# Network two by seven products: other places for the products in the spare bank, the output sums, the copies of TI and the loads of W7

## The chip, the cores and the metric

The kernel runs on one core of a Trainium2 chip. The metric is device time in microseconds (us). Engines: PE is TensorE (matmuls), DVE is VectorE, ACT is ScalarE, POOL is GpSimd, SP is the engine whose queue issues nearly all DMAs. SBUF is the on-chip memory and PSUM, which the matmuls write, is used here as eight banks of 128 x 512 float32.

## What is computed

Three parts follow each other: a two-dimensional Fourier transform (its real part), a gated network ("network one") and a second network ("network two"):

```
def _moe2_ref(x, w_in, w_out):
    h = x @ w_in                  # 12288 x 256 @ 256 x 2048
    g = h - np.tanh(h)
    return (g @ w_out)            # 12288 x 2048 @ 2048 x 256
```

The change touches network two and the last steps of network one ahead of it.

## The kernel before

Tokens are taken in 12 blocks of 1024 (`n` = 0 to 11), the 2048 hidden columns in 8 steps of 256 (`q` = 0 to 7). In a step the product with `w_in` is a 2 x 2 block product done with seven products in place of eight (the names `a11`, `a12`, `a22`, `s1` to `s4`). Each product of a 128 x 128 weight with 512 tokens in float32 is three matmuls (`mm3`, lines 395 to 397). The product with `w_out` is taken two steps at a time: for an even step (`seven` in the code, called a seven step here) it is again seven products, with sums of the weight `W7` and of the activations; for an odd step it is eight plain ones (`whole`, with the weight `WO`), six matmuls for each of the blocks "11", "12", "21" and "22". Block 0 uses an older routine (`quad`, with plain products only); blocks 1 to 11 use `step`.

The eight PSUM banks: `x0` and `x1` (used in turn by the steps), `z`, `w` (a step's work) and four outputs `o00`, `o01`, `o10`, `o11`. In a step the bank `x` of the other parity is first still read by the step before (DVE turns its content into operands, the rows `m<-x` and `s<-x`), and then free until the next step begins: `apart` uses it as spare bank (tile `k`) for those of the seven products that belong to two outputs. Four of the seven (`a11`, `s1`, `s2`, `s3`) go there; `add` then puts `k` into an SBUF sum `acc` (a copy by ACT for the first one of a block, line 1015, a DVE addition after that, line 1017), and the next step's first product can start in the bank when that is done. The other three go straight to an output bank (`direct`). After the last step of a block, `joined` adds the four sums up on POOL (lines 1024 to 1027) and `ready` adds an output bank to each and stores it (lines 1031 to 1034). A block's last products are made in step 0 and step 1 of the next block: `joined` at the end of step 0, `ready` in step 1, right behind the last product of the outputs.

Every engine takes its instructions in the order of the code. Work that belongs to no step (the split of the next block's operands, the loads and splits of weights) is written into numbered slots, four for a step (`at`), and `fill` puts the next slot's work into the program at four places of each step; slot `16 * NP` is the first of network two. Names of that work: `weights2` loads `w_in` (tile `wf`), splits it into `TI` and `w_out` into `WO`, and stores `TI` in DRAM (`ti<-TI`), from where `stream` loads it again for later blocks; `seven` loads and splits `W7`; `left2` loads the next block's activations (`xk<-spill`).

## Time and profile before

| what | value |
|---|---|
| time, median of 3 runs | 1729.41 us (1728.98 to 1732.79) |
| profiled execution, its own time | 1735.3 us |
| span in the profiled execution | 1733.5 us |
| PE busy | 1653.2 us, 95% |
| DVE busy | 1284.5 us, 74% |
| ACT busy | 1214.2 us, 70% |
| POOL busy | 1101.9 us, 64% |
| mean granted TensorE clock | 0.98 |

A busy PE counts overlapped matmuls, each with a modelled end; whether it runs at its rate is read from the distance of the starts. "Idle before" an instruction is the time that its engine had nothing to do ahead of it, and the name behind the arrow is what ended it.

### The profile page before, as it was taken

To read this page: it belongs to the slowest core of one execution; us is meant where nothing else is said; L and a number is where in the kernel's file an instruction comes from. 1 tells how busy PE (TensorE), PEld (TensorE's weight loads), DVE (VectorE), ACT (ScalarE), POOL (GpSimd) and SP (SyncE) were. 2 spreads that over 40 slices of the span, in tenths; PEclk is the share of its full clock that TensorE was granted. 3 is DMA by queue.
4 is the path that set the end of the run, shared out by engine and by line. 5 is a ranking of instruction groups with operands and counts; after the bars stand their busy time and mean duration, and the time that the engine had idled before them with its cause. 6 is when DMAs were issued, how large, how long until landed. Compare 5 with 4: busy or idle time off the path is not lost.

```text
span 1733.5 us, 22370 instructions
## 1 busy us (share of the span) xinstructions
PE 1653.2 (95%) x7346; PEld 1331.8 (77%) x7346; DVE 1284.5 (74%) x1979; ACT 1214.2 (70%) x2333; POOL 1101.9 (64%) x913
## 2 busy tenths in 40 slices
PE   8999999999999999899998999999999999999997
PEld 7978888888888887677776777777767777777775
DVE  7987888888988976667676767666666666676766
ACT  5887777777777766777676767676757676767664
POOL 1166666667767664957575757585757575667644
PEclk9999999999999999999999999999999999999999
DMA  9610111121111134352323232323232333323220
GB/s 330 158 52 26 44 61 44 43 68 49 50 37 43 55 132 136 134 197 86 131 88 112 89 130 86 134 85 121 98 114 98 103 107 106 109 88 131 80 94 25
DMA packets 58341, 167.97 MB, mean 97 GB/s; under 512 B 6752, under 2 KB 14944, under 8 KB 58224
## 3 DMA queue, kind: packets, MB, share of 16 engines
q1 hardware_dynamic: 56640, 162.08, 27.3%
q0 software_dynamic: 1440, 4.46, 1.5%
q8 instruction: 58, 0.95, 0.2%
q14 instruction: 59, 0.48, 0.1%
q10 hardware_dynamic: 144, 0.00, 0.0%
HBM read 127.65 MB, written 38.86 MB: 96 GB/s over the span
## 4 chain that ended last, share of the span: by engine, by line
PE 66%; DVE 9%; issue 8%; POOL 7%; ACT 6%; DMA 2%; SPq 1%; POOLq 0%; DVEq 0%; ACTq 0%
PE o L396 9%; PE o L395 9%; PE o L397 9%; PE x L395 6%; PE x L396 5%; PE x L397 5%; PE w L395 2%; PE w L397 2%; PE w L396 2%; DVE acc L1017 2%; PE k L395 2%; POOL a L1058 2%; PE k L397 2%; PE k L396 2%; ACT s L1056 1%
## 5 line engine op out<-in xcount | busy, mean ns | idle before, releaser
L1058 POOL TENSOR_TENSOR a<-g,a 128x512 fp32r<-128x512 f32 x132 | 171.1, 1296 | 195.9 <-ACT a L1056 193.6
L696 POOL TENSOR_TENSOR a<-xk,a 128x512 fp32r<-128x512 f32 x70 | 93.0, 1333 | 149.3 <-ACT a L694 149.3
L1058 POOL TENSOR_TENSOR s<-g,s 128x512 fp32r<-128x512 f32 x132 | 170.8, 1294 | 13.5 <-ACT s L1056 13.5
L395 PE MATMUL o<-m,WO 128*128 128x512 f32 x416 | 162.7, 391 | 0.0
L396 PE MATMUL o<-m,WO 128*128 128x512 f32 x416 | 162.5, 391 | 0.0
L397 PE MATMUL o<-m,WO 128*128 128x512 f32 x416 | 162.4, 390 | 0.0
L1048 ACT ACTIVATE c<-z 128x512 f32<-128x512 f32 x176 | 106.0, 602 | 71.6 <-DVE z L1089 43.4
L696 POOL TENSOR_TENSOR s<-xk,s 128x512 fp32r<-128x512 f32 x94 | 125.4, 1334 | 39.4 <-ACT s L694 36.1
L396 PE MATMUL o<-m,wv 128*128 128x512 f32 x384 | 150.1, 391 | 0.1
L397 PE MATMUL o<-m,wv 128*128 128x512 f32 x384 | 150.0, 391 | 0.0
L395 PE MATMUL o<-m,wv 128*128 128x512 f32 x384 | 150.0, 391 | 0.0
L1158 POOL TENSOR_TENSOR g<-g,g 128x512 f32<-128x512 f32 x88 | 113.6, 1290 | 46.4 <-DVE x L1157 42.3
L1056 ACT CAST a<-g 128x512 fp32r<-128x512 f32 x132 | 82.1, 622 | 60.0 <-DVE g L1094 31.7
L1052 ACT COPY s<-x 128x512 f32<-128x512 f32 x176 | 103.3, 587 | 18.6 <-PE x L397 18.2
L1017 DVE TENSOR_TENSOR acc<-acc,k 128x512 f32<-128x512 f32 x132 | 89.9, 681 | 33.9 <-PE k L397 33.1
L571 ACT ACTIVATE c<-z 128x512 f32<-128x512 f32 x112 | 67.2, 600 | 54.4 <-DVE z L660 53.6
L578 DVE TENSOR_TENSOR m<-z,m 128x512 fp32r<-128x512 f32 x112 | 76.8, 686 | 37.5 <-ACT m L576 37.5
L1056 ACT CAST m<-z 128x512 fp32r<-128x512 f32 x88 | 51.8, 589 | 67.0 <-DVE z L1118 57.2
L395 PE MATMUL x<-a,TI 128*128 128x512 f32 x192 | 81.1, 422 | 14.6 <-ACT acc L1015 8.0
L396 PEld LDWEIGHTS o<-m,WO 128*128 128x128 f32 x416 | 78.3, 188 | 17.1 <-DVE m L578 0.3
L395 PEld LDWEIGHTS o<-m,WO 128*128 128x128 f32 x416 | 78.1, 188 | 17.0
L397 PEld LDWEIGHTS o<-m,WO 128*128 128x128 f32 x416 | 78.2, 188 | 16.8
(278 smaller groups left out, 5436.9 us busy)
## 6 DMA issues: line engine op xcount, KB each, us to landing
TI<-ti SPq DMA_DIRECT2D x88, 896.0 KB, 4.7
spill<-r SPq DMA_DIRECT2D x48, 256.0 KB, 2.6
xk<-spill SPq DMA_DIRECT2D x48, 256.0 KB, 6.3
out<-acc SPq DMA_DIRECT2D x44, 256.0 KB
ti<-TI SPq DMA_DIRECT2D x8, 896.0 KB, 4.7
raw<-w_in SPq DMA_DIRECT2D x32, 128.0 KB, 2.3
cv<-w_out SPq DMA_DIRECT2D x16, 256.0 KB, 3.1
wf<-wf SPq DMA_DIRECT2D x16, 256.0 KB, 5.0
```

What stands on the lines that cost most here:

```text
L395: T.matmul(ps, w[0], m[0], start=start, stop=False, skip_group_check=True)
L396: T.matmul(ps, w[0], m[1], start=False, stop=False, skip_group_check=True)
L397: T.matmul(ps, w[1], m[0], start=False, stop=stop, skip_group_check=True)
L571: A.activation(t, src, ACT.Tanh if ph == 2 else ACT.Relu)
L578: V.tensor_sub(M[blk][:, 1], g, M[blk][:, 0].bitcast(F32))
L696: eng.tensor_sub(S[name][:, 1], src(), S[name][:, 0].bitcast(F32))
L1017: self.V.tensor_add(self.acc[key], self.acc[key], K)
L1048: A.activation(t, src, TANH)
L1052: A.copy(t, src)
L1056: A.copy(M[k][:, 0], src)
L1058: eng.tensor_sub(M[k][:, 1], src, M[k][:, 0].bitcast(F32))
L1158: "+s2": lambda: G.tensor_sub(g("22"), g("22"), g("11")), "+s4": lambda: G.tensor_sub(g("12"), g("12"), g("22")),
```

## The change

In `step`, products in the spare bank are made at other places in the order of PE and their sums at other places in the order of DVE: in a seven step `s3` comes ahead of the step's own `s3` product and `s2` right behind `s1`, in an odd step `a11` comes ahead of the own `s3` and `s1` right behind `s1`. The first sum is a copy by DVE in place of ACT. `joined` stands ahead of the split of `a22` on POOL. The two outputs of `ready` are taken later in step 1: the lower pair behind the first half's operand, the upper pair behind the second half's. The block's first straight products `a22` and `a12` are made in step 2 and no longer in step 1. The three first stores `ti<-TI` move by 7 to 12 slots into block 0, and the loads and splits of `W7` move from slots 10 to 27 of network two to slots 18 to 50, with the tile `wf` of `weights2` in place of one of the four `xt`.

```diff
--- before.py
+++ after.py
@@ -919,7 +919,7 @@
         return u
 
     def weights2(self, slot, q, pool, tag, bufs):
-        a, b = [], []
+        a, b, out = [], [], []
         def load(to, pool, tag, bufs, i):
             def f():
                 to.append(pool.tile([128, TOK], F32, tag=tag, name="wf", bufs=bufs))
@@ -931,21 +931,22 @@
             f, g = self.quad_weights(self.p2a, self.TI[q])
             f(a[0])
             b.append(g)
+            out.append(self.TI[q])
         def wo():
             p, t = (self.p2a, f"WO{q}") if q < 4 else (self.wvp, "wv")
             self.WO[q] = p.tile([128, 2, TOK], F32R, tag=t, name="WO", bufs=1 if q < 4 else 4)
             self.split(self.WO[q], b[1], self.V if q < 2 else self.G)
         def keep():
-            b[0](None)
-            self.nc.sync.dma_start(out=self.ti[q], in_=self.TI[q].rearrange("p s k n -> p (s k n)").bitcast(F32))
-        self.at(slot, load(a, self.p2a, "wf", 1, 4 + q), ti, None, None, None, keep)
+            self.nc.sync.dma_start(out=self.ti[q], in_=out[0].rearrange("p s k n -> p (s k n)").bitcast(F32))
+        self.at(slot, load(a, self.p2a, "wf", 1, 4 + q), ti, None, None, None, lambda: b[0](None))
+        self.at(16 * NP + ((5, 6, 10)[q] if q < 3 else 4 * q - 3), keep)
         self.at(slot + 4, load(b, pool, tag, bufs, 12 + q), None, wo)
 
     def seven(self, slot, q):
 
         src, t, i = [], [], q // 2
         def load():
-            src.append(self.kp.tile([128, TOK], F32, tag="xt", name="wf", bufs=4))
+            src.append(self.p2a.tile([128, TOK], F32, tag="wf", name="wf", bufs=1) if q else self.kp.tile([128, TOK], F32, tag="xt", name="wf", bufs=4))
             for to, at, n in ((0, 128, 128), (128, 0, 128), (256, 256, 256)):
                 self.nc.sync.dma_start(out=src[0][:, to:to + n], in_=self.wf[12 + q, :, at:at + n])
         def first():
@@ -953,7 +954,7 @@
             f, g = self.quad_weights(self.p2b, self.W7[q])
             f(src[0])
             t.append(g)
-        self.at(slot, load, None, first, None, None, lambda: t[0](None))
+        self.at(slot, load, None, first, None, None, None, lambda: t[0](None))
 
     def bank(self, tag, name):
         return self.ps.tile([128, TOK], F32, tag=tag, name=name, bufs=1)
@@ -987,8 +988,6 @@
         t = int(blk[0]) - 1
         for h in range(2):
             self.into(p["n"], t, h, [c[s][:, 128 * h:128 * h + 128] for s in range(2)], p["m"][blk])
-        if p["q"] == 7 and blk in ("21", "12"):
-            self.ready(p["n"], t)
 
     def product(self, w, k):
 
@@ -1012,7 +1011,7 @@
             key = w["n"], k
             if key not in self.acc:
                 self.acc[key] = self.room(self.p2b, "acc", "acc", 6)
-                self.A.copy(self.acc[key], K)
+                self.V.tensor_copy(self.acc[key], K)
             else:
                 self.V.tensor_add(self.acc[key], self.acc[key], K)
         return add
@@ -1026,8 +1025,11 @@
         G.tensor_add(s2, s2, s5)
         G.tensor_add(s5, s5, s3)
 
-    def ready(self, n, t):
-
+    def ready(self, p, t):
+
+        n = p["n"]
+        if n == 0:
+            return
         for h, k in enumerate((("a11", "s2"), ("s3", "s1"))[t]):
             a = self.acc.pop((n, k))
             self.V.tensor_add(a, a, self.C.pop((n, t, h)))
@@ -1066,6 +1068,8 @@
         A.copy(Z, X)
         if seven:
             late("t12", "h21", "g12")
+            if q == 2:
+                self.direct(p2, "a22")
             self.whole(p1, "11")
             P(Z, "a12")
             late("l21", "h12")
@@ -1077,30 +1081,32 @@
             self.whole(p1, "22")
             g = st["11"] = new("g11")
             V.tensor_sub(g, Z, t11)
+            add = self.apart(p2, "s3")
             P(X, "s3")
             hi("a11", g)
             s3 = copied(X)
             lo("a11", g, G)
-            add = self.apart(p2, "s3")
+            add()
             self.fill()
             Wb = self.bank("w", "w")
             P(Wb, "s1", True)
-            add()
+            add = self.apart(p2, "s2")
             V.tensor_add(Z, Wb, s3)
             t22 = bend(Z)
             self.fill()
+            add()
+            if p2 and q == 0:
+                self.joined(n - 1)
             self.direct(p2, "s4")
+            if q == 2:
+                self.direct(p2, "a12")
             g = st["22"] = new("g22")
             V.tensor_sub(g, Z, t22)
             hi("a22", g)
             lo("a22", g, G)
-            add = self.apart(p2, "s2")
             self.fill()
             P(X, "a22")
             P(Wb, "s4")
-            add()
-            if p2 and q == 0:
-                self.joined(n - 1)
         else:
             late("t12", "s3", "s1", "g12", "+s2")
             self.whole(p2, "21")
@@ -1115,28 +1121,31 @@
             if q > 1:
                 self.direct(p1, "a22")
             self.whole(p2, "12")
+            add = self.apart(p1, "a11")
             V.tensor_sub(Z, Z, t11)
             P(X, "s3")
             hi("11", Z)
             s3 = copied(X)
+            add()
             lo("11", Z, V)
             late("hs2", "+s4", "ls2")
-            add = self.apart(p1, "a11")
+            if q == 1:
+                self.ready(p2, 1)
             self.fill()
             Wb = self.bank("w", "w")
             P(Wb, "s1", True)
-            add()
+            add = self.apart(p1, "s1")
             V.tensor_add(Z, Wb, s3)
             t22 = bend(Z)
             late("hs4", "ls4")
             self.fill()
-            if q == 1:
-                self.direct(p1, "a22")
-            add = self.apart(p1, "s1")
-            self.direct(p1, "a12")
+            add()
+            if q > 1:
+                self.direct(p1, "a12")
             V.tensor_sub(Z, Z, t22)
             hi("22", Z)
-            add()
+            if q == 1:
+                self.ready(p2, 0)
             lo("22", Z, V)
             self.fill()
             P(X, "a22")
@@ -1190,8 +1199,8 @@
                     self.p2b = self.ctx.enter_context(self.tc.tile_pool(name="p2b", bufs=1, side="right", reuse_waits="tile"))
                     for j in range(3, 8):
                         self.weights2(z0 + 4 * (j - 2), j, self.kp, "xt", 4)
-                    for j in range(0, 8, 2):
-                        self.seven(z0 + 10 + 2 * j, j)
+                    for j, slot in ((0, 18), (2, 25), (4, 36), (6, 44)):
+                        self.seven(z0 + slot, j)
                 if q == 1 and n + 1 < NP:
                     u = self.left2(n + 1)
                     if n == 0:
@@ -1219,7 +1228,9 @@
         add()
         self.joined(NP - 1)
         self.whole(p, "21")
+        self.ready(p, 1)
         self.whole(p, "12")
+        self.ready(p, 0)
 
 
     def run(self):
```

The places that matter, as the built programs have them. First PE in the second half of a seven step of block 1 (the first of three matmuls of each product alone; `W` and a tile number is the seven-product weight, `k` the spare bank, the last row is the next step's first product). Before:

```order
L395 MATMUL x<-s_7281,TI 128x512
...
L395 MATMUL k<-s_7995,W_7209 128x512
...
L395 MATMUL w<-s_7244,TI 128x512
...
L395 MATMUL o_7695<-s_8046,W_7209 128x512
...
L395 MATMUL k<-s_8027,W_7209 128x512
...
L395 MATMUL x<-a_7097,TI 128x512
...
L395 MATMUL w<-s_7389,TI 128x512
...
L395 MATMUL x<-a_6977,TI 128x512
```

The same half in the changed program:

```order
L395 MATMUL k<-s_7995,W_7625 128x512
...
L395 MATMUL x<-s_7247,TI 128x512
...
L395 MATMUL w<-s_7216,TI 128x512
...
L395 MATMUL k<-s_8032,W_7625 128x512
...
L395 MATMUL o_7676<-s_8050,W_7625 128x512
...
L395 MATMUL x<-a_7071,TI 128x512
...
L395 MATMUL w<-s_7359,TI 128x512
...
L395 MATMUL x<-a_6965,TI 128x512
```

The first product in the spare bank has moved ahead of the step's own third product, the second one ahead of the straight one; nine matmuls now stand between the second and the next step's first product, where six stood.

Second, DVE from step 0 into step 1 of a block from the third on (`acc<-acc,o` are the output sums of the block before, `s<-x,s` is the operand that empties the bank of step 0). Before:

```order
L1147 TENSOR_TENSOR w<-w,s 128x512
L1150 TENSOR_TENSOR x<-x,c 128x512
L1157 TENSOR_TENSOR g_9081<-g_9081,x 128x512
L1157 TENSOR_TENSOR x<-x,g_9108 128x512
L1154 TENSOR_TENSOR g_9142<-w,c 128x512
L1033 TENSOR_TENSOR acc<-acc,o_8438 128x512
L1033 TENSOR_TENSOR acc<-acc,o_8504 128x512
L1058 TENSOR_TENSOR s_9158<-x,s_9158 128x512
L1033 TENSOR_TENSOR acc<-acc,o_8446 128x512
L1033 TENSOR_TENSOR acc<-acc,o_8480 128x512
```

In the changed program:

```order
L1163 TENSOR_TENSOR g_9142<-w,c 128x512
L1060 TENSOR_TENSOR s_9154<-x,s_9154 128x512
L1125 TENSOR_TENSOR z<-z,c 128x512
L1014 COPY acc<-k 128x512
L1060 TENSOR_TENSOR m_9184<-z,m_9184 128x512
L1035 TENSOR_TENSOR acc<-acc,o_8469 128x512
L1035 TENSOR_TENSOR acc<-acc,o_8501 128x512
L1138 TENSOR_TENSOR z<-w,s 128x512
L1014 COPY acc<-k 128x512
L1145 TENSOR_TENSOR z<-z,c 128x512
L1035 TENSOR_TENSOR acc<-acc,o_8473 128x512
L1035 TENSOR_TENSOR acc<-acc,o_8477 128x512
```

The output sums stood ahead of and around the operand that empties the bank; now they stand behind it, two and two, with the copies out of the spare bank among them.

Third, the queue of SP in block 0 (`wf<-wf` of 128 x 512 loads weights, of 128 x 128 and 128 x 256 the weights of a `W7`; `ti<-TI` is 896 KB). Before:

```order
L940 DMA ti<-TI 128x1792
L926 DMA wf<-wf 128x512
L940 DMA ti<-TI 128x1792
L499 DMA wf<-cvb 128x512
L926 DMA wf<-wf 128x512 x2
L843 DMA spill<-r 128x512 x4
L940 DMA ti<-TI 128x1792
L926 DMA wf<-wf 128x512 x3
L940 DMA ti<-TI 128x1792
L950 DMA wf<-wf 128x128 x2
L950 DMA wf<-wf 128x256
L916 DMA xk<-spill 128x512 x4
```

In the changed program:

```order
L499 DMA wf<-cvb 128x512
L926 DMA wf<-wf 128x512 x2
L843 DMA spill<-r 128x512 x4
L926 DMA wf<-wf 128x512
L940 DMA ti<-TI 128x1792 x2
L926 DMA wf<-wf 128x512 x2
L940 DMA ti<-TI 128x1792 x2
L916 DMA xk<-spill 128x512 x4
L926 DMA wf<-wf 128x512 x2
```

The first two stores have moved behind the spills of network one's last block, the third one behind the fourth; the loads of `W7` no longer stand there.

## Rows read from the trace of the kernel before

**Rows 1.** Busy time by stretch: us, each engine's busy us (instructions), granted clock, DMA share, GB/s.

```profile
160.00:620.00 460.00, 460.00 (x2026) 378.67 (x2025) 396.42 (x590) 346.36 (x643) 309.91 (x247) 1.00 0.16 53
630.00:747.00 117.00, 107.26 (x441) 84.14 (x441) 77.96 (x115) 78.98 (x149) 81.48 (x92) 0.96 0.43 146
747.00:846.78 99.78, 94.20 (x401) 73.81 (x399) 69.12 (x107) 70.62 (x131) 64.46 (x51) 1.00 0.31 105
846.78:1644.92 798.14, 753.19 (x3133) 592.92 (x3133) 544.59 (x829) 542.31 (x999) 538.12 (x424) 0.97 0.31 107
1644.92:1733.50 88.58, 77.06 (x315) 60.23 (x315) 55.91 (x85) 48.77 (x89) 41.47 (x33) 0.93 0.18 64
```

**Rows 2.** PE's groups of instructions from 846.7 to 1644.8 us: busy, mean ns | idle before.

```profile
L395 PE MATMUL x<-a,TI 128*128 128x512 f32 x144 | 61.1, 425 | 10.6 <-ACT acc L1015 6.6 <-DVE acc L1017 1.8
...
L395 PE MATMUL k<-s,W 128*128 128x512 f32 x108 | 47.2, 437 | 7.9 <-ACT acc L1015 3.7 <-DVE acc L1017 2.1
...
L395 PE MATMUL k<-a,W 128*128 128x512 f32 x36 | 15.2, 424 | 26.4 <-DVE s L1058 26.4
```

**Rows 3.** Timeline of steps 0 and 1 of block 6: start, us, engine, instruction [idle before].

```profile
1185.86 0.68 DVE L1058 TENSOR_TENSOR m<-x,m 128x512 fp32r<-128x512 f32 x1
...
1188.70 0.39 PE L395 MATMUL k<-s,W 128*128 128x512 f32 x1
...
1189.58 0.69 DVE L1017 TENSOR_TENSOR acc<-acc,k 128x512 f32<-128x512 f32 x1 [0.91 <-PE k L397]
...
1191.75 0.69 DVE L1094 TENSOR_TENSOR g<-z,c 128x512 f32<-128x512 f32 x1 [0.74 <-ACT c L1048]
...
1192.36 0.68 DVE L1017 TENSOR_TENSOR acc<-acc,k 128x512 f32<-128x512 f32 x1
...
1193.09 0.50 PE L395 MATMUL x<-a,TI 128*128 128x512 f32 x1 [0.15 <-DVE acc L1017]
...
1194.42 1.30 POOL L1024 TENSOR_TENSOR acc<-acc 128x512 f32<-128x512 f32 x1
...
1198.55 1.26 POOL L1027 TENSOR_TENSOR acc<-acc 128x512 f32<-128x512 f32 x1
...
1199.84 1.28 DVE L1033 TENSOR_TENSOR acc<-acc,o 128x512 f32<-128x512 f32 x2 [3.52 <-POOL acc L1027]
...
1201.04 0.68 DVE L1058 TENSOR_TENSOR s<-x,s 128x512 fp32r<-128x512 f32 x1
...
1201.78 0.50 PE L395 MATMUL k<-a,W 128*128 128x512 f32 x1 [2.92 <-DVE s L1058]
...
1202.83 0.63 PE L395 MATMUL w<-s,TI 128*128 128x512 f32 x1
```

**Rows 4.** ACT's timeline in the last steps of network one and in block 0.

```profile
652.41 0.51 ACT L429 CAST TI<-wf 128x384 fp32r<-128x384 f32 x1 [3.63 <-DMA wf<-wf]
...
694.23 0.51 ACT L429 CAST TI<-wf 128x384 fp32r<-128x384 f32 x1 [1.84 <-DMA wf<-wf]
...
720.89 0.62 ACT L429 CAST W<-t 128x512 fp32r<-128x512 f32 x1 [2.71 <-POOL t L519]
...
731.17 0.51 ACT L429 CAST W<-wf 128x384 fp32r<-128x384 f32 x1 [4.44 <-DMA wf<-wf]
```

**Rows 5.** PE's timeline in block 0.

```profile
723.05 0.50 PE L395 MATMUL x<-s,TI 128*128 128x512 f32 x1 [2.90 <-ACT s L593]
...
732.70 0.50 PE L395 MATMUL x<-a,TI 128*128 128x512 f32 x1 [1.46 <-ACT s L645]
```

**Rows 6.** Timeline of SP's queue at the third `TI`.

```profile
645.32 0.32 SPq L940 DMA_DIRECT2D ti<-TI  x1
...
646.20 2.12 SPq L926 DMA_DIRECT2D wf<-wf  x2
```

**Rows 7.** Part 6 of the page: DMA issues, KB each, median us to landing.

```profile
ti<-TI SPq DMA_DIRECT2D x8, 896.0 KB, 4.7
```

**Rows 8.** DVE's copies out of an output bank in block 1.

```profile
L1177 DVE COPY o<-o 128x512 f32<-128x512 f32 x2 | 1.4, 681 | 0.0
```

## The prediction

> **What bounds the kernel now.** I read the busy time by stretch first. In network one PE starts 2026 matmuls in 460.00 us with all of it busy and a granted clock of 1.00, so a matmul costs 0.227 us when nothing waits [rows 1]. That is the floor, and every later stretch is held against it: starts times 0.227, and what the stretch took beyond. The end of network one and block 0 (630 to 747 us) took 117.00 us for 441 matmuls, 16.9 beyond the floor. Block 1 with the first step of block 2 took 99.78 us for 401, 8.7 beyond. The nine blocks from 846.78 to 1644.92 took 798.14 us for 3133 (348 a block), 86.9 beyond, or 9.66 a block. The last stretch took 88.58 us for 315, 17.1 beyond [rows 1]. Block 11's share in that is 9.66 less the long wait described below, which lies just ahead of the stretch (3.1): 6.6. The other 10.5 is the end, where sums and stores run with no matmul left; the change keeps its order and I leave it. So 119 us of PE time are open, in small pieces.
>
> Then I read what stands ahead of PE's groups in the nine blocks [rows 2]. Idle time is in three: `x<-a`, the first product of a step, 10.6 us; `k<-s`, a second product in the spare bank, 7.9; `k<-a`, the first one of an odd step, 26.4. That is 4.99 us a block, all for a bank that is not yet emptied. The other 4.67 follow from the waits: a first matmul after a wait takes 0.50 us and not 0.39, and after the long wait matmuls of 0.63 us show the lower clock [rows 3], which is why the stretch has 0.97.
>
> The timeline of steps 0 and 1 of a block shows both kinds [rows 3]. Small: the sum of the second product in the spare bank starts at 1192.36 and ends at 1193.04; the next step's first matmul, in the same bank, starts at 1193.09. Long: POOL does `joined` from 1194.42 to 1199.81; DVE stands before the output sums until 1199.84 (3.52 us idle), only then makes the operand `s<-x` (1201.04) that empties the bank of step 0, and the product `k<-a` starts at 1201.78 after 2.92 us of idle PE.
>
> **The change part by part.** *Seven step.* From the first matmul in the bank to the start of its sum it takes 0.88 us (1188.70 to 1189.58), and the sum 0.69 [rows 3]. The first product goes three matmuls earlier, to 1188.02; the bank was emptied by `m<-x` at 1186.54, so 1.48 us are to spare. Its sum runs to 1189.59, the second product can follow at 1190.06 (nine matmuls after the first): 0.47 to spare. The second sum then falls into the 0.74 us in which DVE waits for ACT ahead of `g` at 1191.75 [rows 3]: 1191.01 to 1191.70. The next step is due twelve matmuls after 1190.06, at 1192.78: the bank is free 1.08 earlier. The wait at `x<-a` is gone, 1.18 idle us a block and its restarts.
>
> *Odd step.* Six matmuls stood from the first product's start to the second's (1.36 us) against 0.88 + 0.69 = 1.57 for product and sum: short by the 0.2 that `k<-s` shows four times a block (7.9 / 36). With nine there are 2.04, again 0.47 to spare.
>
> *First sums on DVE.* ACT's copies stand behind most of the idle time at `x<-a` and `k<-s` (6.6 + 3.7 of 18.5 [rows 2]). A copy by DVE out of a bank took 0.68 us [rows 8], an addition 0.68 [rows 3]: these steps become like the others, and I add nothing.
>
> *Output sums.* `joined` can start when the second sum is done, 1191.75 in place of 1194.42, since that sum is earlier and the split of `a22` now stands behind it; it lasts 5.39 us and ends at 1197.14. Step 1 starts at 1192.78. The copy out of its first spare product begins 21 matmuls and 0.88 later, at 1198.43, the operand behind it is done by about 1199.7, and only then do the output sums stand: they find `joined` done 2.5 us before. The 3.52 and with them the 2.92 go.
>
> What is late next: DVE has 17 operations in step 1, at 0.6 us from start to start, against 13 in another odd step. The lower output pair delays `z<-w,s` to about 1200.9 and the copy out of the second spare product to 1202.2, while step 2, 39 matmuls after 1192.78, is due at 1201.6: a wait of 0.6. Behind it POOL works off `joined` and five operations of 1.3 (to about 1203.5) before ACT can cast `s4`; the cast of "22" stands behind that on ACT and the copy into `z` behind both, so `z<-a12` of step 2 waits about 0.9. With two restarts 1.75 us stay in each block (an estimate from these rows). Bounds: 0.5 if POOL's end does not reach ACT; 5.5 if the two grow into one wait as long as 2.92 with the lower clock behind it. I take 1.75, because waits of 0.6 and 0.9 are nearer to the 1.46 of block 0 [rows 5] than to 2.92.
>
> Gain of the blocks: nine times 9.66 - 1.75 = 71.2; block 11: 6.6 - 1.75 = 4.9; block 1 and the start of block 2: 8.7 less 1.75 and less 1.5 for block 1's first waits, which the change does not touch, 5.4. Together 81.5.
>
> *Stores and loads in block 0.* A store `ti<-TI` of 896 KB goes out at 645.32, loads behind it at 646.20 [rows 6], and ACT's cast of `TI` waits 3.63 us until 652.41 [rows 4]. The store takes 4.7 us to landing [rows 7]; with it behind the load the wait is gone. How much of an ACT wait comes through to PE: 2.71 at 720.89 gave 2.90 at 723.05, 4.44 at 731.17 gave 1.46 at 732.70 [rows 4, 5]. A long one costs its length and 2 to 3 us of lower clock, so I take 6 for the first and 5 for the one at 723, and 1.8 for the one at 732.70. The last two come from `W7` (casts `W<-t` and `W<-wf`), which now stands later, when POOL and SP have less to do: +6 +6.8. Against it: the cast of 694.23, which waits 1.84 today [rows 4], gets 640 KB more in front of its load (the third store in, a `W7` out), up to 640 / 896 x 4.7 = 3.4 us: -3. And the second `W7` is loaded right behind the last store with some 5 us until its cast, less than store and load need: -1.5 (0 to -4). Net 8.3, between -2 and 13.
>
> The Trainium skill ("DMA: Bandwidth & Descriptors", section "Queues, rings and completion order") says that each DMA engine takes the descriptors of one queue in ring order. By that, the two losses stand as taken; were loads free to overtake, the net would be 12.8. The wait at 652.41 behind the store agrees with the rule.
>
> **Sum.** 81.5 + 8.3 = 89.8. The profiled execution took 1735.3 us, of which its span is 1733.5; less 89.8 that is 1645.5. It lies 5.9 above the median of the runs, 1729.4. Part of the gain is low clock after long waits, which can differ between executions and which the median has less of, so I do not take all of the 5.9 off again: 1643.
>
> **The rivals.** *A, the margins do not hold.* 0.47 us at two places of a step is little, and ACT also casts for the next block there. If half of the eight steps keep a wait like that of 1193.09 (0.31 after 1192.78, when it was due, and 0.11 for a first matmul of 0.50), that is 1.7 a block over eleven blocks: 1661. For it: today's small waits are of just that size. Against: 460 us of network one without any wait.
>
> *B, the long wait only moves.* If step 1 keeps 5.5 us a block, DVE being the engine that step 2 waits for: 10 x 3.75 more, 1680. For it: the 17 operations. Against: step 2 has 48 matmuls for ten DVE operations, so the lag is caught up.
>
> *C, block 0 gains nothing* since stores pushed in front of loads take what leaving them out elsewhere gives: 1651; at the bound of -2, 1653.
>
> *D, slower.* The first spare product now needs its bank 0.68 us earlier in every step. If DVE's operand out of the bank came later than that, PE would wait at each of the 88 steps. It decides when it costs 89.8 / 88 = 1.0 us a step; with 1.48 to spare in a seven step the operand would have to come 2.5 us later than it does. Then 1735 and more.
>
> *E, the change does not do what it says*: the output sums wait for POOL at their new place too, because `joined` starts no earlier; 1.1 to 2.9 us of the long wait stay, some 1700.
>
> **How the numbers follow.** Chances: forecast 0.55 (its own range 1631 to 1655), A 0.18, B 0.12, C 0.08, D 0.03, E 0.04. The range that leaves no more than 2 in 10 out reaches from 1629 (step 1 at its lower bound, and 13 from block 0) to 1672, between A and B. No change is what lies within 0.2% (about 3.5 us, what a measurement of this kernel can tell): 0.02; faster 0.95; slower 0.03.
>
> **What would show it.** A stretch of nine blocks should take 727 us and not 798, with a granted clock of 1.00. No wait of PE on `acc` at `x<-a` and `k<-s`; none at `k<-a`; DVE's output sums with no idle time behind POOL; waits of 0.5 to 1 us at the first products of step 2 only. `x<-a` or `k<-s` waits on `acc` in other steps mean A, a wait of over 2 us at step 2 with matmuls of 0.63 behind it B, ACT waiting for `wf<-wf` longer than 4 us in block 0 C. The forecast is wrong if PE's floor is not reached although its waits are gone.

## The result and the profile after

The changed kernel takes 1650.74 us (median of four runs, 1649.88 to 1651.2) against 1731.1 us of the kernel before (four runs as well; the 1729.41 ahead is the median of the first three of them): a ratio of 0.9533, with a 95% interval from 0.9514 to 0.9552. The forecast was 1643 us, between 1629 and 1672. The profiled execution took 1649.88 us (span 1648.1) where that of before took 1735.3.

Both traces hold the same number of matmuls, 7346, so stretches can be cut at the same matmul numbers and compared. I cut at the first `z<-a` of block 0, the first matmul of block 1, the `k<-a` of the long wait in blocks 2 and 11, and the last matmul. (In the new order the matmul with the number of that `k<-a` is the `x<-s` three matmuls behind `k<-a`.) Busy time by stretch of the kernel before, cut so (us, then PE, PE's loads, DVE, ACT, POOL, granted clock, DMA share, GB/s):

```profile
649.56:752.40 102.84, 92.94 (x378) 72.62 (x378) 67.03 (x99) 70.03 (x131) 66.27 (x79) 0.95 0.44 151
752.40:846.78 94.38, 89.17 (x378) 69.98 (x378) 65.72 (x101) 66.47 (x123) 64.00 (x51) 1.00 0.30 102
...
1644.92:1723.83 78.91, 76.67 (x315) 60.23 (x315) 53.44 (x81) 48.77 (x89) 37.87 (x31) 0.96 0.17 59
```

The third stretch is that of [rows 1], 798.14 us. The same four stretches of the changed kernel:

```profile
648.16:746.33 98.17, 90.41 (x378) 72.17 (x378) 65.31 (x99) 67.23 (x126) 57.46 (x67) 0.95 0.47 166
746.33:835.47 89.14, 87.58 (x378) 70.44 (x379) 67.28 (x103) 66.11 (x123) 69.63 (x61) 1.00 0.33 113
835.47:1564.20 728.73, 716.47 (x3133) 586.02 (x3132) 566.94 (x865) 526.14 (x964) 538.19 (x424) 1.00 0.34 117
1564.20:1638.38 74.18, 72.08 (x315) 58.72 (x314) 56.57 (x87) 47.34 (x86) 39.96 (x33) 1.00 0.19 65
```

So block 0 gained 4.67 us, block 1 5.24, the nine blocks 69.41, block 11 with the end 4.73: 84.05. The other 1.40 lies ahead of block 0, in network one, whose products are the same. The traces of all the kernels here differ by up to 4.9 us at that place, so it counts as no gain of the change. In the nine blocks the granted clock went from 0.97 to 1.00, and of the 9.66 us a block beyond the floor 1.95 are left (86.9 - 69.4 = 17.5 over nine).

What is left there are two waits. PE's groups of the nine blocks that have idle time ahead of them, against [rows 2]:

```profile
L395 PE MATMUL w<-s,TI 128*128 128x512 f32 x144 | 57.0, 396 | 6.2 <-DVE z L1138 6.2
...
L395 PE MATMUL z<-a,TI 128*128 128x512 f32 x72 | 29.3, 407 | 6.1 <-ACT z L1068 6.1
```

`x<-a`, `k<-s` and `k<-a`, which had 44.9 us in [rows 2], have none. The two waits of 0.69 and 0.67 cost 1.9 us a block, since the first two matmuls behind each lose another 0.27. The timeline of one block, with the end of step 0 and step 1 as in [rows 3]:

```profile
1153.16 1.29 POOL L1023 TENSOR_TENSOR acc<-acc 128x512 f32<-128x512 f32 x1 [1.02 <-DVE acc L1016]
...
1157.27 1.30 POOL L1026 TENSOR_TENSOR acc<-acc 128x512 f32<-128x512 f32 x1
...
1161.30 1.27 DVE L1035 TENSOR_TENSOR acc<-acc,o 128x512 f32<-128x512 f32 x2
1162.49 0.69 DVE L1138 TENSOR_TENSOR z<-w,s 128x512 f32<-128x512 f32 x1
...
1163.24 0.50 PE L395 MATMUL w<-s,TI 128*128 128x512 f32 x1 [0.69 <-DVE z L1138]
...
1165.07 0.62 ACT L1058 CAST s<-g 128x512 fp32r<-128x512 f32 x1 [1.25 <-POOL g L1167]
1165.60 0.58 ACT L1058 CAST m<-z 128x512 fp32r<-128x512 f32 x1
...
1166.21 0.69 DVE L1060 TENSOR_TENSOR m<-z,m 128x512 fp32r<-128x512 f32 x1 [0.48 <-ACT m L1058]
...
1167.61 0.50 PE L395 MATMUL z<-a,TI 128*128 128x512 f32 x1 [0.67 <-ACT z L1068]
```

`joined` ends at 1158.57, 2.7 us before the first output sum starts, and DVE has no idle time ahead of that sum. The sums stand in front of `z<-w,s`, and PE waits 0.69 for it. On the other side ACT waits for POOL ahead of the cast of `s4`; the cast of "22", DVE's split and the copy into `z` follow one behind the other, and PE waits 0.67.

In block 0 the waits of [rows 4, 5] are gone, and one has come in their place:

```profile
721.23 1.29 POOL L430 TENSOR_TENSOR TI<-t,TI 128x512 fp32r<-128x512 f32 x1
...
722.55 0.32 SPq L940 DMA_DIRECT2D ti<-TI  x1
722.97 2.15 SPq L951 DMA_DIRECT2D wf<-wf  x3
...
727.33 0.51 ACT L429 CAST W<-wf 128x384 fp32r<-128x384 f32 x1 [6.21 <-DMA wf<-wf]
...
729.38 0.80 PE L395 MATMUL x<-s,TI 128*128 128x512 f32 x1 [6.52 <-ACT s L593]
```

The last store waits on SP for POOL's split of `TI`; the load of the second `W7` stands behind it, ACT's cast waits for that load 6.21 us, and PE 6.52.

### The profile page after: what moved, and what is told of

Same layout as the page of the kernel before. It is cut to its first block, busy times and chain, and to the rows that moved or that the text cites. A ratio compares the mean times of both kernels' runs of the same rounds, so it can differ in the third digit from the quotient of the medians.

```text
span 1648.1 us, 22348 instructions
## 1 busy us (share of the span) xinstructions
PE 1606.5 (97%) x7346; PEld 1322.0 (80%) x7346; DVE 1309.6 (79%) x2023; ACT 1194.2 (72%) x2289; POOL 1101.5 (67%) x913
## 4 chain that ended last, share of the span: by engine, by line
PE 85%; DVE 5%; POOL 3%; ACT 2%; issue 2%; DMA 2%; SPq 1%; POOLq 0%; DVEq 0%; ACTq 0%
PE o L396 11%; PE o L397 11%; PE o L395 11%; PE x L395 7%; PE x L396 7%; PE x L397 7%; PE w L395 4%; PE w L396 4%; PE w L397 4%; PE k L395 2%; PE k L397 2%; PE k L396 2%; PE z L395 2%; PE z L397 2%; PE z L396 2%
## 5 line engine op out<-in xcount | busy, mean ns | idle before, releaser
L1016 DVE TENSOR_TENSOR acc<-acc,k 128x512 f32<-128x512 f32 x132 | 90.7, 687 | 21.7 <-PE k L397 21.3
L578 DVE TENSOR_TENSOR m<-z,m 128x512 fp32r<-128x512 f32 x112 | 76.8, 686 | 35.4 <-ACT m L576 35.4
L1058 ACT CAST s<-g 128x512 fp32r<-128x512 f32 x132 | 82.0, 621 | 17.2 <-POOL g L1167 17.0
L430 POOL TENSOR_TENSOR xr<-xt,xr 128x512 fp32r<-128x512 f32 x46 | 60.5, 1322 | 46.6 <-ACT xr L429 46.6
```

Of the source, the lines that this page charges most:

```text
L578: V.tensor_sub(M[blk][:, 1], g, M[blk][:, 0].bitcast(F32))
L1016: self.V.tensor_add(self.acc[key], self.acc[key], K)
L1058: A.copy(M[k][:, 0], src)
```

## The experiments

All are the changed kernel with the edit shown. Times are medians of four or five runs; the ratio is to the kernel before, run beside them. The last four columns are read from one profiled execution of each, cut at the same matmul numbers as above. They repeat to different degrees where the code is the same: block 0 takes 97.0 to 99.4 us in nine kernels (changed, e1 to e4, e6, e7, e10, e11), the nine blocks 728.5 to 728.7 in three (changed, e5, e9).

| kernel | us | ratio, 95% interval | block 0 | block 1 | nine blocks | 11 and end |
|---|---|---|---|---|---|---|
| before | 1731.1 | 1 | 102.8 | 94.4 | 798.1 | 78.9 |
| changed | 1650.7 | 0.9533 (0.9514 to 0.9552) | 98.2 | 89.1 | 728.7 | 74.2 |
| e1 order of sums back | 1689.8 | 0.9752 (0.9728 to 0.9775) | 98.0 | 92.0 | 761.6 | 76.8 |
| e2 output sums and `joined` back | 1694.8 | 0.9787 (0.9758 to 0.9815) | 99.2 | 94.1 | 768.6 | 73.8 |
| e3 `joined` back | 1668.4 | 0.9628 (0.96 to 0.9656) | 97.7 | 89.1 | 744.3 | 75.5 |
| e4 output sums back | 1653.9 | 0.9546 (0.9524 to 0.9568) | 99.4 | 90.9 | 731.1 | 72.8 |
| e10 first sums on ACT | 1683.4 | 0.973 (0.9709 to 0.9752) | 98.5 | 91.2 | 755.7 | 76.4 |
| e9 stores and `W7` back | 1653.6 | 0.9545 (0.9531 to 0.9559) | 103.1 | 87.0 | 728.6 | 74.2 |
| e5 last store later | 1642.5 | 0.9484 (0.947 to 0.9498) | 92.0 | 89.2 | 728.5 | 74.2 |
| e6 lower sums later | 1650.2 | 0.9528 (0.9513 to 0.9542) | 97.0 | 89.2 | 728.7 | 74.2 |
| e7 both waits attacked | 1653.9 | 0.9549 (0.9533 to 0.9565) | 97.1 | 89.2 | 732.1 | 74.6 |
| e11 sums spread | 1642.9 | 0.9496 (0.9475 to 0.9517) | 98.3 | 89.1 | 720.3 | 73.2 |
| e12 spread, last store later | 1635.6 | 0.9454 (0.9433 to 0.9474) | 90.7 | 89.2 | 720.6 | 73.3 |
| e13 same, copy first | 1637.4 | 0.9459 (0.9445 to 0.9472) | 92.5 | 89.2 | 721.9 | 73.4 |

**e1: products and sums in the spare bank in the order of before** (the odd step likewise). With the second sum `joined` goes back to the end of step 0 too, as in e3 below.

```diff
-            add = self.apart(p2, "s3")
             P(X, "s3")
...
             lo("a11", g, G)
-            add()
+            add = self.apart(p2, "s3")
...
-            add = self.apart(p2, "s2")
+            add()
             V.tensor_add(Z, Wb, s3)
...
-            add()
-            if p2 and q == 0:
-                self.joined(n - 1)
...
             lo("a22", g, G)
+            add = self.apart(p2, "s2")
...
             P(Wb, "s4")
+            add()
+            if p2 and q == 0:
+                self.joined(n - 1)
```

> The changed kernel with the products in the spare bank and their sums at the places of before; output sums, stores and W7 stay at their new places. Theory (small waits for a bank, and the long wait behind the output sums, are two things): the small ones come back, 1.18 us idle at x<-a and 0.88 at k<-s in each block with about eight restarts of 0.11, 3 us a block over eleven blocks, 33 us: 1683 (1674 to 1692). The output sums, at their new place in step 1, still find joined done. Rival (the long wait went because the sums' new order lets joined begin 2.7 us earlier): DVE stands before the output sums again, 2 to 3 us a block of PE idle and its lower clock come on top: 1710 to 1735.

It came out in the theory's range: the small waits return, not the long one. 32.8 us go in the nine blocks, 3.6 a block; how much of that is `joined`, this run does not tell. The range was met by another sum: `x<-a` and `k<-s` have 26.4 us of idle time in the nine blocks where 18.5 were expected, and 14.8 of them are one wait that was in neither expectation. Timeline of step 1:

```profile
1179.98 1.27 DVE L1035 TENSOR_TENSOR acc<-acc,o 128x512 f32<-128x512 f32 x2
1181.17 0.68 DVE L1014 COPY acc<-k 128x512 f32<-128x512 f32 x1
...
1181.90 0.50 PE L395 MATMUL k<-s,W 128*128 128x512 f32 x1 [1.65 <-DVE acc L1014]
```

The first copy stands behind the output sums, and with six matmuls between the two products PE waits 1.65 for it. In the new order the same copy runs ahead of the sums.

**e2, e3, e4: the output sums and `joined`.** e2 puts both back, e3 `joined` alone, e4 the sums alone.

```diff
             self.whole(p2, "21")
+            if q == 1:
+                self.ready(p2, 1)
...
             self.whole(p2, "12")
+            if q == 1:
+                self.ready(p2, 0)
...
-            if p2 and q == 0:
-                self.joined(n - 1)
...
             P(X, "a22")
             P(Wb, "s4")
+            if p2 and q == 0:
+                self.joined(n - 1)
```

> The changed kernel with joined at the end of step 0 and the output sums directly behind the last products into their banks, both as before; the new order of products and sums stays. Theory: POOL does the split of a22 first and joined ends 2.8 us later (1161.4 in the time of the changed kernel's trace); DVE, which could start the output sums at 1157.8, stands there 3.6 us, and PE waits about 2.9 us a block at k<-a with matmuls at the lower clock behind it: 4 to 6 us a block more over ten blocks, 1690 to 1712. Rival (the new order of products and sums alone did away with the long wait): under 1660.

> The changed kernel with joined alone at the end of step 0, behind the split of a22 on POOL; the output sums stay late in step 1. Theory: joined ends at about 1161.4 in place of 1158.6, and the first output sum starts at 1161.30 today: at most 0.1 to 0.3 us of DVE a block, 1650 to 1656. Rival (the earlier start of joined is what removed the long wait): 1680 and more, with DVE idle behind POOL ahead of the output sums.

> The changed kernel with the output sums alone directly behind the last products into their banks, as before; joined stays early in POOL's row. Theory: joined ends at 1158.57 and DVE could start the sums at 1157.8, so it stands 0.8 us and its operand out of the bank comes 2.1 us later; in the kernel before 4.8 us of delay gave 2.92 of wait, so 1.9 are free: 0.2 us of wait a block or none, and the two waits of today (1.95 us a block) become smaller, since fewer sums stand in their way: 1640 to 1656. Rival (the late place of the output sums is what removed the long wait): 1680 to 1710.

e2 is as the theory had it in time and cause. The wait is longer than the 2.9 us expected, and matmuls of 0.63 follow it:

```profile
1184.96 1.28 DVE L1035 TENSOR_TENSOR acc<-acc,o 128x512 f32<-128x512 f32 x2 [3.50 <-POOL acc L1026]
...
1186.90 0.50 PE L395 MATMUL k<-a,W 128*128 128x512 f32 x1 [4.05 <-DVE s L1060]
...
1188.59 0.63 PE L395 MATMUL w<-s,TI 128*128 128x512 f32 x1
```

e4 came out in its range by another sum: PE waits 1.39 at `k<-a`, not 0.2 or less, but the two waits of the changed kernel are gone, and the block is hardly longer. DVE stood 0.83 for POOL, as worked out.

```profile
1161.85 1.29 DVE L1035 TENSOR_TENSOR acc<-acc,o 128x512 f32<-128x512 f32 x2 [0.83 <-POOL acc L1026]
...
1163.79 0.50 PE L395 MATMUL k<-a,W 128*128 128x512 f32 x1 [1.39 <-DVE s L1060]
```

In e3 both expectations failed: 1668.4 lies between them. `joined` is done just in time for the sums, as the theory said; DVE has no idle time there. The loss is elsewhere:

```profile
1169.72 1.28 DVE L1035 TENSOR_TENSOR acc<-acc,o 128x512 f32<-128x512 f32 x2
...
1174.84 0.62 ACT L1058 CAST s<-g 128x512 fp32r<-128x512 f32 x1 [2.58 <-POOL g L1167]
...
1177.38 0.50 PE L395 MATMUL z<-a,TI 128*128 128x512 f32 x1 [1.99 <-ACT z L1068]
```

In the changed kernel `joined` fills time in which POOL waits for its next operand; behind that operand everything on POOL comes 1.3 us later, ACT's wait ahead of the cast of `s4` goes from 1.25 to 2.58, and PE's at `z<-a` from 0.67 to 1.99. Over nine blocks: both moved 69.4 us gained, only `joined` moved 67.1 (e4), only the output sums 53.9 (e3), neither 29.5 (e2). Either move alone does away with most of the long wait.

**e10: the first sum of each block copied by ACT.**

```diff
-                self.V.tensor_copy(self.acc[key], K)
+                self.A.copy(self.acc[key], K)
```

> The changed kernel with the first sum of each output block copied out of the spare bank by ACT, as before, and not by DVE. Theory (the prediction gave this part of the change nothing): two copies of 0.68 leave DVE's row in step 1, two of 0.6 enter ACT's, and what PE waits for at step 2 stays within 0.5 us a block: 1646 to 1655. Rival (ACT's row is the tighter one there, its copies stand behind products and hold back the casts behind them, as 6.6 and 3.7 us of idle time in nine blocks showed in the kernel before): 1656 to 1668.

Neither held: 32.6 us slower than the changed kernel, 27.0 of them in the nine blocks. Timeline of step 1:

```profile
1182.00 0.62 ACT L1058 CAST s<-g 128x512 fp32r<-128x512 f32 x1 [1.25 <-POOL g L1167]
1182.53 0.58 ACT L1014 COPY acc<-k 128x512 f32<-128x512 f32 x1
...
1183.16 0.50 PE L395 MATMUL x<-a,TI 128*128 128x512 f32 x1 [2.02 <-ACT acc L1014]
```

The rival had the copies hold back the casts; it is the other way round. The copy stands behind the cast that waits for POOL, and hands that wait to the bank and so to PE. By its duration ACT would be the better engine (0.58 against DVE's 0.68). The Trainium skill ("PSUM — Partial Sum Buffer", section "Engine vs sequencer instructions") says that ScalarE's queue is strictly first in, first out; these rows agree, the copy 0.53 us behind the cast. The Trainium skill ("VectorE: DVE Perf Modes", section "Specifications") has ScalarE as the engine closer to PSUM. It gives no time there; the copy out of PSUM was 0.10 us shorter on ACT, and here that does not decide.

**e9: stores of `TI` and loads of `W7` as before** (the main diff's first three pieces and its slots of `seven` undone).

```diff
+            b[0](None)
             self.nc.sync.dma_start(out=self.ti[q], in_=self.TI[q].rearrange("p s k n -> p (s k n)").bitcast(F32))
-        self.at(16 * NP + ((5, 6, 10)[q] if q < 3 else 4 * q - 3), keep)
...
-                    for j, slot in ((0, 18), (2, 25), (4, 36), (6, 44)):
-                        self.seven(z0 + slot, j)
+                    for j in range(0, 8, 2):
+                        self.seven(z0 + 10 + 2 * j, j)
```

> The changed kernel with the stores of TI and the loads of W7 at the places of before; products, sums and outputs stay new. Theory (the prediction's gain of 8.3 us in block 0 was nearly eaten by the second W7 behind the last store): from 630 to 740 us the kernel before lost 16.9 us beyond the floor up to 747 us and the changed one about 14, so 3 us are lost: 1651 to 1657, with ACT waiting for wf near 650 again and without the wait of 6.5 us of PE near 729. Rival (the moved stores gained what was predicted and block 1 lost it): 1658 to 1662.

As the theory had it in size: 2.9 us, though the intervals of the two ratios overlap. The stretches show two parts, each clear of its spread. Block 0 loses 4.95, all that it had gained (103.1 against 97.0 to 99.4), and block 1 gets 2.13 back (87.0 against 89.1 to 89.2). Most of the latter is a wait in block 1 of the changed kernel that e9 has not:

```profile
791.09 1.30 POOL L430 TENSOR_TENSOR W<-t,W 128x512 fp32r<-128x512 f32 x1
792.34 1.28 POOL L1060 TENSOR_TENSOR a<-g,a 128x512 fp32r<-128x512 f32 x1
...
793.67 0.50 PE L396 MATMUL o<-a,W 128*128 128x512 f32 x1 [1.17 <-POOL a L1060]
```

The third and the fourth `W7` were moved from block 0 into block 1; the last split of the fourth now stands on POOL ahead of an operand that PE needs at once.

**e5: the last store one slot later, behind the load of the second `W7`.**

```diff
-        self.at(16 * NP + ((5, 6, 10)[q] if q < 3 else 4 * q - 3), keep)
+        self.at(16 * NP + ((5, 6, 10)[q] if q < 3 else 4 * q - 3 + (q == 7)), keep)
```

> The changed kernel with one number changed: the last store of TI is issued one slot later, behind the load of the second W7. Theory (the load's three transfers lie behind 896 KB of store): they land about as soon as loads of such a size did elsewhere, 2 to 3 us after their issue, ACT's cast comes near 725 and not at 727.33, and PE's wait of 6.52 at 729 shrinks to 3 to 4.5 with less of low clock behind it: 1643 to 1648. Rival (the load is late by its own issue, behind POOL's split, and not by the store): 1649 to 1652.

8.2 us faster than the changed kernel by the medians, a little more than the theory gave; in the profiled executions block 0 gains 6.2 (98.17 to 91.95), and the other stretches are the same. The theory's reason was too narrow: more than the store's transfer, its wait held the load. Timeline at the same place:

```profile
718.39 1.27 SPq L951 DMA_DIRECT2D wf<-wf  x3
...
723.24 0.52 ACT L429 CAST W<-wf 128x384 fp32r<-128x384 f32 x1
...
724.66 0.32 SPq L940 DMA_DIRECT2D ti<-TI  x1
725.30 0.50 PE L395 MATMUL x<-s,TI 128*128 128x512 f32 x1 [0.21 <-ACT s L593]
```

The load goes out at 718.39, 4.6 us earlier than at 722.97; it is there before ACT comes to the cast, which has no idle time ahead of it. Had the transfer been the whole reason, 3 to 4.5 us of wait were expected to stay on PE; 0.21 stayed. The store still goes out only when POOL has finished (724.66). So the rival had the cause half right (the load was late by its issue) and the price wrong. What the transfer cost is not shown, since the edit takes away both. PE's wait of 6.4 to 6.5 us stands in all nine traces with this order of store and load in the new places, and in none of e5, e12, e13.

**e6, e7: the two waits that are left.** e6 moves `ready(p2, 1)` alone (the lower sums behind `z<-w,s`); e7 is all.

```diff
             late("l12")
+            if q == 2:
+                p2["late"]["hs4"]()
+                p2["late"]["ls4"]()
...
-            if q == 1:
-                self.ready(p2, 1)
             self.fill()
...
             V.tensor_add(Z, Wb, s3)
+            if q == 1:
+                self.ready(p2, 1)
             t22 = bend(Z)
-            late("hs4", "ls4")
+            if q > 1:
+                late("hs4", "ls4")
...
             hi("22", Z)
+            lo("22", Z, V)
             if q == 1:
                 self.ready(p2, 0)
-            lo("22", Z, V)
```

> The changed kernel with the lower pair's output sums in step 1 put behind z<-w,s, so that PE's first wait of a block (0.69 at w<-s, for DVE) has no cause any more. Theory (both waits of a block hang on one chain: POOL is busy without a break from joined at 1153.16 to the operand of s4 at 1165.07, and step 2's z waits for what ACT does behind it): the first wait goes and the second grows by as much, 0.67 to about 1.6: 1648 to 1653. Rival (two separate waits, 0.96 us a block each with its restart): ten blocks by 0.96 less, 1639 to 1643.

> As the kernel before this one in the list, and ACT's cast of s4 (with its split) goes out of step 1 behind the first casts of step 2, the upper pair's output sums behind the split of 22. Theory: ACT and DVE no longer wait for POOL ahead of step 2's z, both waits of a block are gone, ten times 1.9 us less: 1630 to 1636. Rival (DVE's row is full, 17 operations in step 1, and the wait only moves to the next product): 1640 to 1650.

e6 gave the time that the theory gave, for another reason. The second wait did not grow (0.56); the first moved on by a few matmuls, to the bank whose copy now stands behind the sums:

```profile
1162.32 1.27 DVE L1035 TENSOR_TENSOR acc<-acc,o 128x512 f32<-128x512 f32 x2
1163.51 0.68 DVE L1014 COPY acc<-k 128x512 f32<-128x512 f32 x1
...
1164.25 0.50 PE L395 MATMUL x<-a,TI 128*128 128x512 f32 x1 [0.81 <-DVE acc L1014]
```

In e7 ACT no longer waits for POOL ahead of that `z<-a`, which waits for nothing. The wait of 0.81 at `x<-a` stays, and one of 0.89 stands at `o<-m,WO`, whose bank the upper output sums have not yet read. My theory that the chain over POOL and ACT sets both waits is refuted; the rival holds (DVE's row is full there), though it gave 1640 to 1650 and 1653.9 was measured.

```profile
1166.39 1.27 DVE L1035 TENSOR_TENSOR acc<-acc,o 128x512 f32<-128x512 f32 x2
...
1167.12 0.50 PE L395 MATMUL o<-m,WO 128*128 128x512 f32 x1 [0.89 <-DVE acc L1035]
```

**e11, e12, e13: the four output sums one by one.** `ready` gets a parameter for which of its two sums it issues; the cast of `s4` moves as in e7. e12 adds the edit of e5; in e13 the second sum stands behind the fourth. ("The two kernels before" in the first text are e6 and e7.)

```diff
             add = self.apart(p1, "a11")
+            if q == 1:
+                self.ready(p2, 1, (0,))
             V.tensor_sub(Z, Z, t11)
...
             V.tensor_add(Z, Wb, s3)
+            if q == 1:
+                self.ready(p2, 1, (1,))
...
             hi("22", Z)
             if q == 1:
-                self.ready(p2, 0)
+                self.ready(p2, 0, (0,))
             lo("22", Z, V)
+            if q == 1:
+                self.ready(p2, 0, (1,))
```

> The changed kernel with the four output sums apart: the first into the 0.82 us in which DVE waits for ACT ahead of step 1's first z<-z,c, the second behind z<-w,s, the third into the wait for ACT's cast of 22, the fourth behind that split; ACT's cast of s4 goes behind the first casts of step 2. Theory (DVE's row in step 1 is what step 2 waits for, and 0.64 of it can be done in idle time): nothing stands late any more by the rows of the two kernels before, ten times 1.95 us less: 1629 to 1636. Rival (the wait moves once more, as it did in those two): over 1640.

> The output sums apart as in the kernel before this one in the list, and the last store of TI behind the load of the second W7. Theory (two gains at different places add up, 8 us from the store as measured): 1621 to 1628. Rival: the sums' part falls short as told there: 1633 to 1643.

> The last kernel (output sums apart, last store behind the load of the second W7) with the second output sum put behind the fourth, so that the copy out of the spare bank in step 1 comes 0.6 us earlier. Theory (DVE's row still sets the two waits of 0.20 and 0.21 that are left in a block): the wait of step 2's first matmul for that copy goes with its restart, 0.47 a block, and the one for the output sum stays at 0.2: 1628 to 1634. Rival (the wait moves to an operand that now comes later behind the sums): 1634 to 1642.

The theories of e11 and e12 were too good by half, and the rivals' ranges held: 8.5 us of 17.5 are gained in the nine blocks. Two of the four sums found idle time of DVE: the first ahead of `z<-z,c`, the third ahead of `m<-z`, by the idle time (the number behind the second bar) in the nine blocks of e7:

```profile
L1060 DVE TENSOR_TENSOR m<-z,m 128x512 fp32r<-128x512 f32 x72 | 49.6, 690 | 25.3 <-ACT m L1058 24.7
L1128 DVE TENSOR_TENSOR z<-z,c 128x512 f32<-128x512 f32 x37 | 25.9, 700 | 30.2 <-ACT c L1050 30.2
```

and in those of e11:

```profile
L1061 DVE TENSOR_TENSOR m<-z,m 128x512 fp32r<-128x512 f32 x72 | 49.6, 689 | 20.0 <-ACT m L1059 18.8
...
L1131 DVE TENSOR_TENSOR z<-z,c 128x512 f32<-128x512 f32 x37 | 25.9, 699 | 22.4 <-ACT c L1051 22.0
```

The other two sums still stand ahead of work that PE waits for. Two waits of 0.2 are left with their restarts, both for DVE. What e5 and e11 gain nearly adds up (8.2 and 7.8): e12 is the fastest of all, 15.2 us under the changed kernel. In e13 the expectation failed and the rival held: the wait at `x<-a` is gone, that at `o<-m,WO` has grown from 0.21 to 0.27, and one of some 0.15 came at `k<-s`; the nine blocks take 721.9 against 720.6. The wait moves with the sums.

## Why the prediction came out as it did

**The blocks: right.** Nine blocks were to take 727 us, they took 728.7; 1.75 us a block were to stay, 1.95 did. The long wait went by the mechanism given: `joined` starts when the second sum is done, and ends 2.7 us before the output sums stand (2.5 were worked out). The margins of 0.47 hold: no idle time at `x<-a` and `k<-s`, which refutes rival A. No wait of the nine blocks is longer than 0.7 us, so B's long wait did not come either, nor a wait in every step (D). The two waits that stay have the sizes (0.69 and 0.67 for 0.6 and 0.9), and the second has its cause and place. The first is at step 1's `w<-s` and not at step 2's first product, a matter of which reader of DVE's row comes first; e6 moves it to exactly the forecast's place and the time stays.

**"I add nothing" for the first sums on DVE: the sum holds, the term doesn't stand alone.** The prediction put the whole gain of the small waits on the order of products and sums. e10 shows that with ACT's copies the new order keeps 42.4 of 69.4 us, and e1 that with DVE's copies the old order (with `joined` late) keeps 36.6. So 27.0 us hung on an edit that was given nothing. Undoing the order costs 32.8 us in nine blocks, the copies 27.0, output sums with `joined` 39.9, but these can't be added up: `joined` is undone in the first and the last of them. That edits need each other is shown by e2 to e4: `joined` alone costs 15.5, the output sums alone 2.3, both together 39.9. Fixed shares of the gain belong to none of them. The move of the straight products `a22` and `a12` to step 2 was undone in no run.

**Rival E was priced by the wrong path.** It had `joined` starting too late, with the output sums waiting, at some 1700. e3 makes `joined` late; the sums don't wait, POOL's later work does, and the time is 1668. Its 1700 did not follow from its own words either: 1.1 to 2.9 us over ten blocks are 11 to 29 us, 1672 at most without the lower clock behind them.

**Block 0: the term that failed.** "The second `W7` is loaded right behind the last store ...: -1.5 (0 to -4)" was sized by the transfers. PE lost 6.69 beyond the floor at 729.38, 0.37 at the next matmul and some 0.2 at each of the twelve behind it at the lower clock: 9.5, outside the bounds. What was overlooked in its place is that the store itself waits for POOL, and SP issues nothing behind it meanwhile; e5 shows it. By the prediction's sign for rival C (ACT waiting for `wf<-wf` longer than 4 us; it was 6.21) C came in part. The other terms of block 0: the wait at 652.41 gave 5.8 (6 taken), those at 723 to 738 gave 7.9 (6.8 taken), and the loss of 3 at 694.23 did not come (+0.3). Together 4.5 by the single waits and 4.67 by the stretch, for 8.3: about halfway to rival C. The rule of the Trainium skill that the prediction weighed ("DMA: Bandwidth & Descriptors", section "Queues, rings and completion order") is not told apart by these runs: the load that came late had not yet been issued.

**Block 1: right by two errors.** Forecast 5.4, measured 5.24. Taking off 1.75 for the waits of step 2 was wrong, since they lie behind the stretch's end (I counted them in eleven places, there are ten); without it the sum is 7.2, and e9, with the old places of `W7`, has 7.37. The 2.13 that the moved `W7` cost there was in no term.

**The sum.** 84.05 us of the predicted 89.8 came from the stretches, 1.40 from ahead of block 0. That makes 1649.9 for the profiled execution in place of 1645.5. The 2.5 taken off for the medians was not there to take: the median lies 0.9 above the profiled run. Together that is the 7.7 us by which 1643 was too low. The lower bound of 1629 holds less than it says: it is 1643 less eleven times 1.25 for step 1, and with 13 from block 0, 4.7 more, it would be 1624.6. The measured time lies far above both.

## What to carry to other kernels

Edits that bring forward links of one chain (order, engine, start of a sum, place of its reader) are to be priced as a set: here undoing any one of three (order, copies, output sums with `joined`) costs more than a third of the gain in the nine blocks, and either half of the last does most of the work. An operation inherits the wait of whatever stands ahead of it in its engine's row, so for the copy out of a bank the engine with the longer copy, with nothing waiting ahead of it, beat the other by 33 us, and a load behind a store that waits for a split cost 8 us. Where a full row sets the end, moving its work only moved the wait (e6, e7, e13); what helped was work put into the row's idle time (e11).

## What the runs showed of the hardware

The granted clock fell behind the wait of 6.52 us: thirteen matmuls from 729.98 start 0.43 us apart, with a granted clock of 0.50, the lower level of 1.2 GHz.

```profile
729.98:734.90 4.92, 4.92 (x13) 3.86 (x12) 4.13 (x6) 2.64 (x5) 2.20 (x3) 0.50 0.40 166
```

It isn't the length of a wait alone that tells. I counted PE's waits from 1.2 us up, from block 0 on, in all fourteen traces, and whether matmuls of 0.63 us follow (granted clock 0.50 where I read it, as in e3 from 1094.80 and in e10 from 1267.60 us):

| wait, us | where | followed by matmuls of 0.63 |
|---|---|---|
| 1.2 to 1.7 | 10 in e1 and e4 each at one place of a block, and others | 0 of 30 |
| 1.97 to 2.04 | e3 and e10, one a block | 7 of 20 |
| 2.29 and 2.83 | e9, block 0 | 0 of 2 |
| 2.90 to 2.97 | before | 11 of 11 |
| 3.9 to 6.5 | block 0, and one a block in e2 | 21 of 21 |

At some 2 us the same wait at the same place of a block was followed by them in one block and not in the next: in e10 seven follow one wait of 2.04 us, and none another.

The fourteen traces, whose products are the same up to there, reach the first `z<-a` of block 0 anywhere between 648.16 and 653.01 us. So 1 to 2 us between two single executions mean nothing by themselves, and in block 0 not even by the stretch, which differs by 2.4 us where the code is the same.
